# Linear attention and a gated MLP on one core: transposed blocks copied as fp32 words, a second identity, wider engine choices and a new order table

## The chip, the cores and the metric

The kernel runs on one core of a Trainium2 chip. The core has five engines with queues of their own: TensorE (PE in the profile) multiplies, VectorE (DVE), ScalarE (ACT) and GpSimd (POOL) work on tiles, and SyncE (SP) issues nearly all DMAs here. TensorE writes only to PSUM, eight banks of which serve as one ring; DVE and ACT read PSUM, POOL does not. The metric is the device time in microseconds; less is better.

## The reference

Four batches, eight heads, 768 steps, head size 48. First a gated recurrence per head, then a two-layer MLP whose second half is normalised and mixed over the sequence:

```python
for t in range(S):
    state = alpha[:, :, t, :, None] * state + np.einsum('bhd,bhe->bhde', k[:, :, t], v[:, :, t])
    y[:, :, t] = np.einsum('bhd,bhde->bhe', q[:, :, t], state)
# x = y as (4, 768, 384)
h = np.maximum(x @ w_in, 0.0)                      # w_in: 384 x 1024
u, v = (h[..., :512].copy(), h[..., 512:].copy())
v_n = (v - mean(v)) / np.sqrt(var(v) + 1e-06)      # over the last axis
v_s = np.einsum('ts,bsd->btd', w_spatial, v_n) + b_spatial[None, :, None]
out = (u * v_s) @ w_out                            # w_out: 512 x 384
```

## The kernel before, in words

The sequence of a batch is cut into six chunks of 128 steps, 24 chunks in all, numbered i. Within a chunk the recurrence becomes matmuls. The first eight chunks are handled in four pairs (`pair`, numbered j: chunks 2j and 2j+1, interleaved by parity `par`), the other sixteen one by one (`first`). The steps of a pair, by the names that the table of operations gives them:

- `ac`, `kc`, `qc`, `vc`: four loads, 384 KB each for a pair, 192 KB for a single chunk.
- `lnp`: ACT takes the logarithm of alpha (L443). `cump` j par: two matmuls on a triangle matrix sum the logarithms (L452). `einvp` and `eexpp`: ACT takes exp of minus the sum and of the sum (L460, L469).
- `ktp` (k times the first, L474, POOL before) and `qtp` (q times the second, L481, DVE).
- `tr` k/q: four transposes through a PSUM bank against the identity `ident` (L502). `ev` k/q: that bank is copied to SBUF as `kqT` (L198 on ACT, L200 on DVE: both lines belong to the helper `copy`).
- `sc`: score matmuls (L574), `m`: DVE multiplies the scores with a mask (L585), `ya` and `y`: matmuls to the chunk's output (L601, L614).
- `updq`, `z`, `S`, `sb`: the state of 128x192 fp32. TensorE makes the update (L544), DVE adds the old state (`z`, L328 and L330), `S` multiplies with the decay (L335), `sb` copies it to bf16 (POOL).
- `xs`, `xt`, `xe`: the output is copied to SBUF, transposed (L365 for pairs, L389 for single chunks) and copied out of PSUM as `xT`, the MLP's input.

Single chunks have the same steps as `ln`, `cum`, `einv`, `eexp`, `kt`, `qt`, `trk`, `ev`, `sc`, `m`, `y` (L651 to L773). The MLP per batch: `v` (six tiles of three 512-column matmuls, then relu to `v_sb`), `bn` (mean and variance), `rs` (one over the deviation), `vn` (the normalised tile, L916), `u` (eight groups of three matmuls, then relu), `s` (eight groups of six 384-column matmuls on `vn` and the transposed `w_spatial`, then DVE adds the bias, L967), `g` (product with u, L980), `o` (six groups of four matmuls) and `st` (the stores). All big matmul groups are issued at L819. Weights come as fp32 (`raw_w`) and are cast to bf16 by `cast`; `w_spatial` is transposed by `wt` and copied by `we`.

The order of everything is written out by hand: `PLAN` lists one word per operation, with a letter for the engine and the operation's number, and `replay` emits the operations in that order. Each engine runs its own instructions strictly in that order, SP its DMAs too; semaphores make an instruction wait for its inputs and for its PSUM bank. Each operation has a table of engines it may be given to (`ENGINES` and dictionaries beside the calls of `op`). Numbers behind a PE word (`P118:512:512:192`) are filler: that many columns of fp32 matmul on a constant tile `junk`, put into the bank just ahead of the real matmuls (L188).

Before, the first words issue the loads `ac` 0, `ac` 2, `kc` 0, `vc` 0, `qc` 0, `qc` 2, `kc` 2, `w_in` 1, `vc` 2, `ac` 4; a load is numbered by the first chunk of its pair, so that `ac` 2 belongs to pair 1. The first `cump` is that of pair 1. Filler of 512, 512 and 192 columns stands ahead of it, 512, 512, 512 ahead of the first `tr`, 504 ahead of the first `sc` and 512 ahead of the first `ya`.

Of the kernel before, what the change touches and what calls it, by code (L numbers as in the profile page):

```python
# [36 lines left out]
class Slot:  # L37
# [7 lines left out]
    "S": {"POOL": 0.5},  # L45
    "sb": {"POOL": 0.73, "DVE": 0.95},
    "vn": {"DVE": 0.42},
    "xe": {"ACT": 0.4},
# [9 lines left out]
D0 S49 Q50 D7 D13 S109 Q110 G47 Q48 D11 S51 Q52 G9 D3 S55 Q56 D1 G8 D15 D17 G14 D6 D4 D2 D12 G16 S53 Q54 A57 S113 Q114  # L58
G18 A117 P118:512:512:192 S111 Q112 P68 A119 P262 A69 P58 S19 Q20 P264 G71 A59 P128 A120 A60 G61 S115 Q116 A70 D62
A129 D72 A265 D5 S178 Q179 A263 D122 A130 P126:512:512:512 D132 S180 Q181 G131 P76 P74 P64 P66 D75 G63 A65 D77 G73 D67  # L60
D127 G121 P89:504 P134 S182 Q183 D90 P136 P78 A135 D91 A137 P86 S184 Q185 G133 D80 A23 P124 D88 P149 A79 A125 G81 D87
A123 S322 Q323 G22 D83 A186 P92:512 D151 G82 P146 D93 G21 P96 P187 D150 A97 G84 P197 S24 Q25 A188 P94 D148 P138 G85
A95 D147 A189 G190 P98 S326 Q327 P100 A198 D191 A99 G200 A199 D140 P103 S324 Q325 A101 D201 G202 P195 A139 A192 D102
P203 G141 P193 A104 P205 P207 G142 D143 A194 D196 A206 P152 G144 D204 S29 Q30 D105 A330 S382 Q383 G145 P153 P157 P215
A154 D158 G10 P212 A208 A106 D209 P155 P341 D213 A156 G210 P159 P331 D214 A160 P161 A332 D216 G28 P172 A342 D217 G211
A333 A343 D335 G27 P218 A173 D345 G26 A162 P223 P219 D174 P349 A224 P339 S33 Q34 G334 P170 A220 S328 Q329 D350 P225
D163 P221 S384 Q385 P166 G344 A226 A222 P164 D167 A175 P337 P230 D171 A165 A338 D107 P227 D177 A231 D108 S386 Q387
P168 A390 D176 D340 A228 D32 P347 A169 P238 D31 A348 D229 P247 A239 P244 P362 S37 Q38 A245 P236 D248 A246 D249 G35
P240 D364 A237 S424 Q425 P242 A346 D363 G336 A241 P250 G36 D232 P391 A252 P351 A393 A243 D251 S426 Q427 P253 A233 D353
P270 A392 D234 P266 S428 Q429 A352 A255 D235 G354 P274 D254 A395 P275 D356 G355 D396 P271 G394 D276 P267 D272 S388  # L70
# [54 lines left out]
def kernel(  # L125
# [76 lines left out]
    def relu(eng, out, in_):  # L202
        if eng == "ACT":
            nc.scalar.activation(out=out, in_=in_, func=AF.Relu)  # L204
        else:
            ENG[eng].tensor_scalar_max(out=out, in0=in_, scalar1=0.0)
# [953 lines left out]
```

## Time and profile before

| | us |
|---|---|
| median of three runs | 141.43 (141.38 to 141.93) |
| span of the profiled execution | 144.3 |
| TensorE busy in it | 136.8 (95%) |
| VectorE busy | 118.7 (82%) |
| ScalarE busy | 106.8 (74%) |
| GpSimd busy | 86.8 (60%) |

The page gives no other time for the profiled execution than its span, which runs from its first to its last instruction and is 2.9 us above the median of the runs. Busy time of an engine is the union of its instructions' spans; matmuls are pipelined, so that a row of 326 ns for a 384-column matmul says how long one takes from start to end, not how far apart two of them start.

### The profile page before, as it was taken

To read this page: it belongs to the slowest core of one execution; us is meant where nothing else is said; L and a number is where in the kernel's file an instruction comes from. 1 tells how busy PE (TensorE), PEld (TensorE's weight loads), DVE (VectorE), ACT (ScalarE), POOL (GpSimd) and SP (SyncE) were. 2 spreads that over 40 slices of the span, in tenths; PEclk is the share of its full clock that TensorE was granted. 3 is DMA by queue.
4 is the path that set the end of the run, shared out by engine and by line. 5 is a ranking of instruction groups with operands and counts; after the bars stand their busy time and mean duration, and the time that the engine had idled before them with its cause. 6 is when DMAs were issued, how large, how long until landed. Compare 5 with 4: busy or idle time off the path is not lost.

```text
span 144.3 us, 4963 instructions
## 1 busy us (share of the span) xinstructions
PE 136.8 (95%) x1915; PEld 84.2 (58%) x1915; DVE 118.7 (82%) x289; ACT 106.8 (74%) x278; POOL 86.8 (60%) x152
## 2 busy tenths in 40 slices
PE   7799999799799999999999999999999999999990
PEld 3334766656465765676556665665657666555560
DVE  7015798899999969899999999999979897987940
ACT  3473479899895879899997789998797698861031
POOL 6856179892709979981249789511599687002820
PEclk9999999999999999999999999999999999999998
DMA  4999999929899989999899899799999241090055
GB/s 108 321 326 351 282 250 325 344 58 259 181 269 191 300 164 182 205 181 214 169 211 222 175 174 185 152 204 196 212 239 227 66 172 55 0 354 28 5 191 191
DMA packets 89000, 28.64 MB, mean 198 GB/s; under 512 B 83728, under 2 KB 87440, under 8 KB 88976
## 3 DMA queue, kind: packets, MB, share of 16 engines
q1 hardware_dynamic: 88944, 28.32, 79.5%
q8 instruction: 15, 0.25, 0.7%
q14 instruction: 9, 0.07, 0.1%
q0 software_dynamic: 32, 0.00, 0.0%
HBM read 23.60 MB, written 4.72 MB: 196 GB/s over the span
## 4 chain that ended last, share of the span: by engine, by line
PE 78%; DVE 8%; ACT 5%; DMA 3%; issue 3%; SPq 0%; ACTq 0%; DVEq 0%
PE bank L819 47%; PE bank L188 4%; DMA ac<-in_alpha_dram 3%; PE bank L710 3%; PE bank L452 2%; PE bank L502 2%; PE bank L745 2%; PE bank L574 2%; DVE ptm L756 2%; PE bank L773 2%; PE bank L731 2%; PE bank L544 1%; DVE ptm L585 1%; PE bank L657 1%; PE bank L601 1%
## 5 line engine op out<-in xcount | busy, mean ns | idle before, releaser
L819 PE MATMUL bank<-w_spT,vn 128*128 128x384 bf16 x192 | 36.3, 326 | 0.1
L980 POOL TENSOR_TENSOR gT<-vsb,uT 128x384 bf16<-128x384 f32 x28 | 25.7, 927 | 11.7 <-DVE vsb L967 11.2
L335 POOL TENSOR_TENSOR state<-state,bc 128x192 f32<-128x192 f32 x20 | 10.3, 513 | 21.4 <-DVE state L328 6.2
L819 PEld LDWEIGHTS <-vn 128*128 128x128 bf16 x192 | 17.1, 97 | 10.2 <-issue 0.2
L756 DVE TENSOR_TENSOR ptm<-bank,mask 128x512 bf16<-128x512 f32 x32 | 20.8, 682 | 1.0 <-ACT xT L198 1.0
L819 PE MATMUL bank<-xT,w_in 128*128 128x384 bf16 x96 | 19.4, 326 | 0.0
L967 DVE TENSOR_TENSOR vsb<-bank,bsp_bc 128x384 f32<-128x384 f32 x31 | 16.7, 554 | 3.2 <-PE bank L819 2.8
L819 PE MATMUL bank<-w_in,xT 128*128 128x512 bf16 x72 | 18.8, 379 | 0.0
L198 ACT COPY kqT<-bank 128x512 bf16<-128x512 bf16 x24 | 13.6, 590 | 6.9 <-PE bank L502 4.4
L819 PE MATMUL bank<-w_out_sb,gT 128*128 128x384 bf16 (+1 forms) x100 | 18.4, 320 | 0.1
L681 POOL TENSOR_TENSOR kt<-kc,binv 128x384 bf16<-128x384 f32 x13 | 12.0, 927 | 6.6 <-ACT bc L676 2.7
L200 POOL CAST sbd<-state 64x192 bf16<-64x192 f32 x40 | 13.6, 341 | 2.1
L884 DVE BATCH_NORM_STATS2 stats<-v_sb 128x6 f32<-128x512 bf16 x20 | 13.6, 681 | 0.5 <-ACT v_sb L204 0.5
L204 ACT ACTIVATE v_sb<-bank 128x512 bf16<-128x512 f32 x20 | 11.9, 608 | 1.6 <-PE bank L819 1.6
L198 ACT CAST x_sb<-bank 128x384 bf16<-128x384 f32 x21 | 10.2, 493 | 3.5 <-PE bank L773 2.7
L819 PEld LDWEIGHTS <-w_in 128*128 128x128 bf16 x96 | 8.7, 97 | 6.0
L188 PE MATMUL bank<-junk 128*128 128x512 f32 (+2 forms) x16 | 11.1, 838 | 1.1 <-DVE halves_of L264 1.1
L200 DVE COPY kqT<-bank 128x512 bf16<-128x512 bf16 x24 | 9.2, 415 | 3.1 <-PE bank L502 2.3
L819 PEld LDWEIGHTS <-gT 128*128 128x128 bf16 x100 | 8.7, 97 | 5.1 <-POOL gT L980 0.2
L204 ACT ACTIVATE uT<-bank 128x384 bf16<-128x384 f32 x23 | 11.3, 495 | 0.3 <-PE bank L819 0.2
L198 ACT COPY xT<-bank 128x192 bf16<-128x192 bf16 (+1 forms) x27 | 9.1, 378 | 2.4 <-PE bank L365 1.5
L585 DVE TENSOR_TENSOR ptm<-bank,mask 128x512 bf16<-128x512 f32 x16 | 10.2, 682 | 0.7 <-PE bank L574 0.4
(128 smaller groups left out, 285.2 us busy)
## 6 DMA issues: line engine op xcount, KB each, us to landing
ac<-in_alpha_dram SPq DMA_DIRECT2D x16, 192.0 KB, 3.9
kc<-in_k_dram SPq DMA_DIRECT2D x16, 192.0 KB, 4.2
qc<-in_q_dram SPq DMA_DIRECT2D x16, 192.0 KB, 4.0
vc<-in_v_dram SPq DMA_DIRECT2D x16, 192.0 KB, 3.8
raw_w<-in_moe_w_spatial_dram SPq DMA_DIRECT2D x3, 768.0 KB, 4.5
out_dram<-raw_w SPq DMA_DIRECT2D x11, 192.0 KB, 2.0
out_dram<-o_sb SPq DMA_DIRECT2D x9, 192.0 KB, 1.9
ac<-in_alpha_dram SPq DMA_DIRECT2D x4, 384.0 KB, 5.5
```

What stands on the lines that cost most here:

```text
L188: nc.tensor.matmul(out=flat[:, 0:cols].rearrange("p (a b) -> p a b", a=4), lhsT=junk, rhs=junk[:, None, 0:n].to_broadcast([128, 4, n]), st ...
L198: nc.scalar.copy(out=out, in_=in_)
L200: ENG[eng].tensor_copy(out=out, in_=in_)
L204: nc.scalar.activation(out=out, in_=in_, func=AF.Relu)
L335: ENG[eng].tensor_tensor(out=st["state"], in0=st["state"], in1=st["bc"][:, :, None].to_broadcast([128, HP, D]), op=ALU.mult)
L585: nc.vector.tensor_tensor(out=st[f"ptm{par}"][:, s], in0=st[f"pt{s}{par}"], in1=mask2[:, par], op=ALU.mult)
L681: ENG[eng].tensor_mul(out=k_blocks(kt3)[:, :, :, 0:D], in0=quad(st["kc"]), in1=st["binv"])
L756: nc.vector.tensor_tensor(out=st["ptm"][:, s], in0=st[f"pt{s}"], in1=mask4, op=ALU.mult)
L819: return lambda ps: nc.tensor.matmul(out=out(ps), lhsT=lhsT(), rhs=rhs(), start=start, stop=stop)
L884: nc.vector.bn_stats(out=stats, in_=d["v_sb"][:, tt, :])
L967: nc.vector.tensor_tensor(out=hold["vs"], in0=ps[:, 0:TH], in1=bsp_bc[:, th, :], op=ALU.add)
L980: ENG[eng].tensor_tensor(out=bt[b]["gT"][:, dsl, cols], in0=hold["vs"], in1=bt[b]["uT"][:, dsl, cols], op=ALU.mult)
```

## The change

Six things change at once.

1. `copy_pairs`: where a transposed bf16 block leaves PSUM (`ev`, `xe`, `we`) and the engine is ACT, input and output are viewed as fp32, so that a 128x512 block is copied as 128x256 words. On DVE the copy is as before.
2. `ident_q`: a permuted identity, made by one more POOL copy behind `ident`. `xt` of the pairs transposes against it, so that the columns come out in the order in which `xT` keeps them, and `xe` of the pairs copies straight instead of with a stride.
3. `ENGINES`: `S` may also go to DVE, `vn` also to POOL (two POOL instructions, a 128x1 and a 128x512 one), `xe` of pairs and `v` also to DVE.
4. `b_sp_sb` no longer has a tile of its own but lies in `w_spT`.
5. `c_id` issues the extra copy.
6. `PLAN` is another table with the same 1156 words.

By the new table `vn` is 16 times on POOL and 8 times on DVE (24 on DVE before), `S` 12 times on DVE and 8 on POOL (20 on POOL before), `ev` 38 times on ACT and 10 on DVE (24 and 24 before), `v` 5 times on DVE (all 24 on ACT before), `ktp` 3 of 8 times on DVE, `g` 25 times on POOL and 6 on DVE (28 and 3), `vb`/`vbp` 10 times on POOL (14 before), the casts of `w_sp` 4 times on POOL and 2 on ACT (3 POOL, 2 DVE, 1 ACT). The loads come in the order `ac` 2, `ac` 0, `qc` 0, `kc` 0, `qc` 2, `vc` 0, `kc` 2, `ac` 4, `qc` 4, `vc` 2, `w_in` 1, `kc` 4. Filler is 3008 columns in 24 pieces (3768 in 8 before): 1152 columns in six pieces ahead of the first `cump` (pair 1's again), the rest in pieces of 64 to 256 columns, 640 of it in six pieces between that `cump` and the first `tr`. The order of the first DVE steps after the loads is `ktp` 0, four `qtp`, a bias copy, `ktp` 1, then `z`, `S`, `z` and the masks of pair 0; ACT's is the eight exponentials (a bias copy among them), a `vb` cast, and `ev`.

```diff
 ENGINES = {
     "kt": {"POOL": 0.9, "DVE": 0.47},
     "vb": {"POOL": 0.48, "ACT": 0.42, "DVE": 0.27},
-    "S": {"POOL": 0.5},
+    "S": {"POOL": 0.5, "DVE": 0.35},
     "sb": {"POOL": 0.73, "DVE": 0.95},
-    "vn": {"DVE": 0.42},
-    "xe": {"ACT": 0.4},
+    "vn": {"DVE": 0.42, "POOL": 0.75},
+    "xe": {"ACT": 0.4, "DVE": 0.3},
...
 PLAN = """
-D0 S49 Q50 D7 D13 S109 Q110 G47 Q48 D11 S51 Q52 G9 D3 S55 Q56 D1 G8 D15 D17 G14 D6 D4 D2 D12 G16 S53 Q54 A57 S113 Q114
-G18 A117 P118:512:512:192 S111 Q112 P68 A119 P262 A69 P58 S19 Q20 P264 G71 A59 P128 A120 A60 G61 S115 Q116 A70 D62
+S109 Q110 D0 D2 G47 Q48 D13 D15 G14 S49 Q50 D17 D3 D6 D12 D5 G18 S53 Q54 D4 D1 D11 A117 S51 Q52 G9 G16
+P118:384:320:64:128:128:128 A57 S113 Q114 A119 A120 S55 Q56 P58:64:128 A59 P128:128 P68 A60 S111 Q112 D61 P262 A69 A70
...
+    def copy_pairs(eng, out, in_):
+
+        copy(eng, *((out.bitcast(FP32), in_.bitcast(FP32)) if eng == "ACT" else (out, in_)))
+
...
+    ident_q = consts.tile([128, 128], BF16, name="ident_q")
...
-    b_sp_sb = consts.tile([1, S], BF16, name="b_sp_sb")
     wsp_nat = [None] * NT
     w_spT = consts.tile([128, NT, NT, 128], BF16, name="w_spT")
+    b_sp_sb = w_spT[0:1, 0].rearrange("p n t -> p (n t)")
...
-                    nc.tensor.transpose(xv[:, ks, :], st["x_sb"][:, ks, :], ident)
+                    nc.tensor.transpose(xv[:, ks, :], st["x_sb"][:, ks, :], ident_q)
...
-                copy(eng, bt[b]["xT"][:, c].rearrange("p k (t two) -> p k t two", two=2),
-                     st["xv"].rearrange("p k (two t) -> p k t two", two=2))
+                copy_pairs(eng, bt[b]["xT"][:, c], st["xv"])
...
-                        copy(eng, st["kT"][:, par], hold["t"])
+                        copy_pairs(eng, st["kT"][:, par], hold["t"])
...
-                copy(eng, st["kqT"][:, :, 64 * r:64 * r + 64], hold[r])
+                copy_pairs(eng, st["kqT"][:, :, 64 * r:64 * r + 64], hold[r])
...
-                    copy(eng, w_spT[:, tt, :, 64 * r:64 * r + 64], hold[r])
+                    copy_pairs(eng, w_spT[:, tt, :, 64 * r:64 * r + 64], hold[r])
...
-              {"ACT": 0.61 if on_act else 0.48}, None, [made.get(("vn", b - 2, tt))], parts=1)
+              {"ACT": 0.61} if on_act else {"ACT": 0.48, "DVE": 0.6}, None, [made.get(("vn", b - 2, tt))], parts=1)
...
+    def c_id(_):
+        make_identity(nc, ident)
+        nc.gpsimd.tensor_copy(
+            out=ident_q.rearrange("p (t a) -> p a t", a=2), in_=ident.rearrange("p (a t) -> p a t", a=2))
+
+    op(("c_id",), "POOL", 0.5, c_id, prio=-19.0)
```

More of the change, by code (lines that the diff above doesn't have):

```diff
@@ L396, in xe @@
                     tiles(b)
[L397 removed]
+                copy_pairs(eng, bt[b]["xT"][:, c, :, 64 * r:64 * r + 64], to[r])
             made[("xe", i)].append(op(
@@ L517, in ev @@
                                 "p a h c -> p (a h c)").rearrange("p (h c a t) -> p h c a t", a=2, c=2, h=HP)
-                        copy(eng, st["qT"][:, :, :, par, :], hold["t"].rearrange("p h (c t) -> p h c t", c=2))
+                        copy_pairs(eng, st["qT"][:, :, :, par, :], hold["t"].rearrange("p h (c t) -> p h c t", c=2))
                 op(("ev", nm, j, par), EV, None, ev,
```

100 lines of the change are left out of this document (49 added, 51 removed).

## The prediction

> **What bounds the kernel now.** I read the page first (busy shares and the chain that ended last), then stretches of time, then the chain itself, and last the timeline and the groups of instructions.
>
> ```profile
> span 144.3 us, 4963 instructions
> PE 136.8 (95%) x1915; PEld 84.2 (58%) x1915; DVE 118.7 (82%) x289; ACT 106.8 (74%) x278; POOL 86.8 (60%) x152
> ...
> PE 78%; DVE 8%; ACT 5%; DMA 3%; issue 3%; SPq 0%; ACTq 0%; DVEq 0%
> ```
>
> ```profile
> 0.00:23.30 23.30, 21.06 (x248) 11.06 (x249) 12.99 (x41) 13.05 (x26) 14.43 (x34) 1.00 0.97 275
> 23.30:40.00 16.70, 14.99 (x264) 9.84 (x263) 15.37 (x36) 14.82 (x38) 12.16 (x22) 1.00 0.79 224
> 40.00:123.50 83.50, 83.24 (x1300) 52.79 (x1299) 77.08 (x184) 71.64 (x195) 55.30 (x92) 1.00 0.87 188
> 123.50:141.10 17.60, 17.54 (x113) 10.46 (x109) 13.30 (x31) 6.94 (x21) 4.90 (x5) 1.00 0.34 124
> ```
>
> The columns of a stretch are its length, busy PE, PEld, DVE, ACT and POOL, the granted clock, the DMA share and GB/s. From 40 us on PE idles 0.3 us in 101: this part is bound by the matmuls, which the change leaves as they are. What can move lies ahead of 40 us. There the chain (start, length, what) shows filler, waits for the first loads, and then DVE:
>
> ```profile
> 1.23 4.23 DMA ac<-in_alpha_dram
> ...
> 6.38 1.44 PE bank L452 x4
> 7.82 0.43 PE bank L848
> ...
> 10.17 4.25 PE bank L188 x6
> 14.43 1.12 PE bank L502 x20
> 15.55 0.90 PE bank L188 x2
> 16.45 0.35 PE bank L574 x16
> ...
> 19.06 1.05 PE bank L188 x2
> 20.11 0.51 PE bank L601 x32
> ...
> 21.25 0.65 PE bank L452 x4
> ...
> 23.48 1.39 PE bank L819 x6
> ...
> 29.46 1.89 DVE ptm L585 x3
> ...
> 35.37 1.84 DVE vn L916 x4
> ...
> 37.54 1.25 DVE w_row L200 x2
> ```
>
> L188 is the filler: 6.2 us on the chain between 10 and 20 us. `ya` of the first pair (L601) starts at 20.11, the first big group (`v`, L819) at 23.48. In 23.3 to 40 us DVE is busy 15.37 of 16.70, and PE loses 1.7 us.
>
> **The change, part by part.** *The start.* The two alpha loads change places:
>
> ```profile
> 1.06 4.42 PE L188 MATMUL bank<-junk 128*128 128x512 f32 x6 [1.06 <-DVE halves_of L264]
> ...
> 4.24 0.84 ACT L443 ACTIVATE la<-ac 128x768 bf16<-128x768 f32 x1 [2.21 <-DMA ac<-in_alpha_dram]
> ...
> 5.48 0.84 ACT L443 ACTIVATE la<-ac 128x768 bf16<-128x768 f32 x1 [0.40 <-DMA ac<-in_alpha_dram]
> ...
> 6.63 1.15 SPq L432 DMA_DIRECT2D kc<-in_k_dram  x1
> ...
> 7.83 1.15 SPq L1084 DMA_DIRECT2D raw_w<-in_moe_w_in_dram  x1
> ```
>
> The first `cump` is pair 1's. Before, pair 1's alpha comes second and `cump` waits to 6.38; after, it comes first, its logarithm ends at 5.08. Six instructions took 4.42 us for 1216 columns, 3.6 ns a column; 1152 columns are 4.2 us, to 5.25. So `cump` starts there, 1.1 us earlier. The steps that follow cost by these groups (busy, mean ns | idle):
>
> ```profile
> L198 ACT COPY kqT<-bank 128x512 bf16<-128x512 bf16 x24 | 13.6, 590 | 6.9 <-PE bank L502 4.4 <-PE bank L710 2.1 <-DVE w_row L200 0.4
> L335 POOL TENSOR_TENSOR state<-state,bc 128x192 f32<-128x192 f32 x20 | 10.3, 513 | 21.4 <-DVE state L328 6.2 <-ACT v_sb L870 4.6 <-DVE vn L916 3.7
> L585 DVE TENSOR_TENSOR ptm<-bank,mask 128x512 bf16<-128x512 f32 x16 | 10.2, 682 | 0.7 <-PE bank L574 0.4 <-issue 0.3
> L200 DVE COPY kqT<-bank 128x512 bf16<-128x512 bf16 x24 | 9.2, 415 | 3.1 <-PE bank L502 2.3 <-ACT o_sb L198 0.5
> L330 DVE TENSOR_TENSOR state<-bank,state 128x192 f32<-128x192 f32 x16 | 5.6, 352 | 0.3
> L198 ACT COPY xT<-bank 128x192 bf16<-128x192 bf16 x19 | 5.3, 335 | 0.9 <-PE bank L389 0.9
> L481 DVE TENSOR_TENSOR qt<-qc,bank 128x384 bf16<-128x384 f32 x8 | 4.2, 545 | 7.1 <-ACT bank L469 7.1
> L460 ACT ACTIVATE binvp<-bank 128x384 bf16<-128x384 f32 x8 | 3.8, 494 | 1.7 <-PE bank L452 1.6
> L198 ACT COPY xT<-bank 128x384 bf16<-128x384 bf16 x8 | 3.7, 480 | 1.5 <-PE bank L365 1.5
> ```
>
> PE: four `cump` at 0.72 (half of 1.44), two bias matmuls at 0.43, 640 columns of filler at 3.6 ns: 6.1 us, so the first transposes stand at 11.35 instead of 14.43. ACT: nine instructions at 0.49 from 6.32, with some 0.7 lost waiting for the fourth `cump`: the last exponential ends at 11.4, the last `qtp` at about 12.0. The first scores need three transposed banks and three ACT copies. A word copy costs what 256 columns cost: between 335 (192) and 480 (384), 0.38 us; the bounds are 0.335 and the 0.590 of today. Banks from about 12.0, copies to 13.1, scores of par 0 to 13.5, of par 1 to 14.0. DVE meanwhile does `z`, `S`, `z` at 0.35 from 13.1, then four masks at 0.68: 14.2 + 2.7 = 16.9. `ya` at 17.0 instead of 20.11: **3.1 us** earlier. `v` stands 3.4 us behind `ya` (23.48 - 20.11) and would come at 20.4, if `w_in` is there:
>
> ```profile
> raw_w<-in_moe_w_in_dram SPq DMA_DIRECT2D x2, 768.0 KB, 6.5
> ```
>
> (KB each, median us from issue to landing.) It is now behind ten loads instead of seven. Issues follow each other every 1.2 us (6.63 to 7.83), so it is issued at 7.83 + 3.6 = 11.4, lands at 17.9, and with its three casts side by side on DVE, ACT and POOL (0.61 to 0.63 each) `v` can start at 18.6: 1.8 us of cover. If the queue makes it 3 us later than that, 1.2 of the 3.1 are lost. I keep 3.1, as the path through `ya` is the later one, with 1.9 as the low end. 1216 columns of filler stand behind the first transpose's place. They cost nothing as long as they lie in waits: between 11.35 and 17.0 the walk gives TensorE some 3.5 us of work (eight banks 1.8, four scores 1.4, the update), so 2 us of waits are there. At the later rate of 0.90 us for 504 columns they are 2.2 us, which would be lost if nothing waited; the old filler of this stretch (6.2 us on the chain) is gone from the walk in exchange.
>
> *23 to 40 us.* Five of the first batch's six `vn` leave DVE for POOL and both `w_row` casts leave it: the chain's 1.84 and 1.25 us. PE's loss there is 1.7 in all; I take **1.0**, between 0 (the masks, 1.89, stay, and `S` is added) and 1.7.
>
> *Whole budgets.* DVE: 16 `vn` less at 0.43 (-6.9), 14 `ev` less (-5.8), 12 `S` more at 0.35 (+4.2), 5 relus of `v` more at 0.68 as for a mask (+3.4), the rest +2.0: about -3 us. ACT: 14 `ev` more at 0.38 (+5.3), 24 shorter by 0.21 (-5.0), 27 `xT` copies shorter by 0.07 to 0.15 (-2.5), five relus less (-3.0), the rest +2: about -3. POOL carries what DVE gave:
>
> ```profile
> L200 POOL CAST w_in<-raw_w 128x512 bf16<-128x512 f32 x5 | 3.0, 610 | 0.1
> L200 POOL CAST w_row<-raw_w 128x768 bf16<-128x768 f32 x3 | 2.5, 826 | 3.2 <-DMA raw_w<-in_moe_w_spatial_dram 2.8 <-DVE w_row L200 0.5
> L980 POOL TENSOR_TENSOR gT<-vsb,uT 128x384 bf16<-128x384 f32 x28 | 25.7, 927 | 11.7 <-DVE vsb L967 11.2
> L916 DVE TENSOR_SCALAR vn<-v_sb,mvs,rstd 128x512 bf16<-128x512 bf16 x24 | 9.2, 430 | 0.9 <-ACT rstd L909 0.6
> ```
>
> No row has this on POOL. One tensor input like the cast: 0.61; the narrow instruction ahead of it as the cast's part that does not grow with columns (0.84 ns a column between 512 and 768), 0.18: 0.79, against 0.43 on DVE. At the two-input rate of L980 (2.41 ns a column) it would be 1.24 + 0.18 = 1.42. I take 0.79, as it reads one tensor. 16 of them are +12.6; 12 `S` less -6.2, `g`, `vb` and `k` products -5.8: POOL stays near 60%. Ahead of the `s` that needs it stand 0.6 us of matmuls (batch 0) to 1.6 (batch 3) behind the last of a row of POOL `vn`; that is the cover. From 40 us on I count nothing gained: PE idles 0.3 us there.
>
> The Trainium skill (GPSIMD Engine Reference, Engine selection) puts elementwise work on VectorE and calls GpSimd about twice as slow with two tensor inputs and near line rate with one. By the one-input half of that rule the 0.79 and the sum stand; if the two per-partition scalars made it an instruction of two inputs, the sum would be that of the slower rival below. No run here shows which.
>
> The extra `ident_q` copy (POOL, 0.3 at most by the cast rows) lies before 7 us, ahead of transposes at 11: free. The bias row in `w_spT` is read before the first `we`: free.
>
> Sum: 3.1 + 1.0 = 4.1. The profiled execution (144.3, 2.9 above the median) becomes 140.2; the median **137.3**.
>
> **Rivals.** *Loads set the pace: smaller gain.* For: the DMA share is 0.97 up to 23.3 us. Against: 1.8 us of cover. With `w_in` 3 us late the start gives 1.9, the sum 2.9: 138.5; without the gain of the second part 139.5.
>
> *The clock stays low: smaller gain.* The same four matmuls (L452) took 1.44 us at 6.38 and 0.65 at 21.25, though the clock column says 1.00 for both; the filler likewise: 4.25 us for six instructions at 10.17, 0.90 for two at 15.55. So TensorE runs at about half speed until between 10 and 15.5 us. In the walk above, transposes (0.22 a bank by 1.12 us for five), scores (0.35 a par) and the update before 17 us are priced fast. If they are slow, three banks and two scores on the path cost 1.4 more, and later filler twice what it should: 1.4 to 2.4 lost, 138.7 to 139.7. The Trainium skill (TensorE: Matmul & The Clock Gate, Part 1) has the array at half rate until a window of some 3.4 us has been busy, and half rate again after an idle one; by that rule filler in small pieces between waits may fail to fill a window, and the time would be the 138.7 to 139.7. The rows agree that it is slow early and fast after 4 us of unbroken filler.
>
> *POOL decides: slower.* In batches 0, 2 and 3 four or five `vn` stand in a row on POOL ahead of `s`. Each 0.1 us above 0.79 delays the last of a row by 0.4. The 4.1 us are gone at 4.1 / (3 x 4) = 0.34 above, at 1.13 us each; at 1.42 it is 3 x 4 x 0.63 = 7.6 lost, 144.9. For: L980's rate; against: the cast's, and a cover of 0.6 to 1.6 us.
>
> *Larger gain.* If all 6.2 us of filler on the chain, the 1.1 of the first load and the 1.7 of the second part went, it were 9.0: 132.4. Half way from the forecast is 134.9.
>
> **How the numbers follow.** Forecast (136.0 to 138.5) 0.45; smaller gain by the loads 0.10, by the clock 0.10 (both to 140.7); larger 0.15; no change 0.05; slower 0.15. Half a per cent is about what a measurement tells from no change. Faster 0.80, same 0.05, slower 0.15. The range 134.6 to 141.6 reaches past the half-way point of the larger gain (0.05 beyond) and leaves out most of the slower case (0.13).
>
> **What would show it.** First L452 at 5.3, first L601 at 17, first L819 by 20.5; ACT `kqT` rows of 256 columns at 0.38; POOL `vn` at 0.6 and a narrow row at 0.2; in 23 to 40 us `vn` and `w_row` off the chain. Wrong, if the chain shows POOL `vn` ahead of L819, or DMA `raw_w` ahead of the first L819.

## The result and the profile after

The changed kernel takes 144.89 us, the median of four executions (144.82 to 145.09), against 141.38 to 141.93 in three of the four executions of before beside it: a ratio of 1.025, with a 95% interval of 1.023 to 1.026. It is slower by 3.4 us, where I forecast 4.1 faster. One plain fact is needed for what follows: executions of the kernel before lie between 141.3 and 145.5 us, and the ratios compare those near the lowest, while the profile on which I built the prediction was of a long one.

From the page of the changed kernel, the busy times and the chain's shares:

```profile
span 143.0 us, 5050 instructions
...
PE 134.6 (94%) x1947; PEld 86.9 (61%) x1947; DVE 118.6 (83%) x280; ACT 102.4 (72%) x291; POOL 93.6 (65%) x165
...
PE 52%; DVE 15%; DMA 10%; POOL 8%; SPq 7%; issue 5%; ACT 0%; POOLq 0%; DVEq 0%
```

The time of this execution, 144.82, is its span and 1.8 us. TensorE's share of the chain fell from 78 to 52%; loads, VectorE and POOL took its place. The first three of the same four stretches as before (length, busy PE, PEld, DVE, ACT, POOL, granted clock, DMA share, GB/s):

```profile
0.00:23.30 23.30, 21.33 (x368) 16.55 (x368) 17.06 (x51) 17.19 (x41) 13.56 (x32) 1.00 1.00 285
23.30:40.00 16.70, 16.26 (x272) 10.52 (x261) 15.00 (x36) 14.88 (x43) 14.64 (x28) 1.00 1.02 296
40.00:123.50 83.50, 80.99 (x1222) 50.43 (x1219) 74.98 (x171) 64.65 (x198) 57.97 (x97) 1.00 0.80 169
```

Before, TensorE was busy 83.24 of the 83.50 us from 40 us on, and I counted nothing there. Now it is idle 2.5 us in that stretch. The chain (start, length, what) shows by whom:

```profile
11.46 6.85 DMA raw_w<-in_moe_w_in_dram
...
20.44 7.87 DMA kc<-in_k_dram
...
30.74 1.55 POOL w_row L200 x2
...
32.64 0.77 POOL vn L929
33.40 0.45 POOL vbp L200
34.19 0.77 POOL vn L929
35.30 0.77 POOL vn L929
36.07 0.78 POOL w_row L200
...
97.59 1.26 POOL vn L929
```

POOL is on it from 30.7 to 36.9 us with 0.1 us between, and again at 97.6. The groups that answer my prices (busy, mean ns | idle before):

```profile
L198 ACT COPY kqT<-bank 128x256 f32<-128x256 f32 x38 | 13.6, 385 | 2.2 <-PE bank L714 1.7 <-DVE vsb L971 0.2 <-DVE qt L485 0.2
L929 POOL TENSOR_SCALAR vn<-v_sb,rstd,nb 128x512 bf16<-128x512 bf16 x16 | 13.1, 818 | 1.6
...
L340 DVE TENSOR_TENSOR state<-state,bc 128x192 f32<-128x192 f32 x12 | 5.5, 461 | 1.1 <-ACT bc L554 0.7
...
L926 POOL TENSOR_SCALAR nb<-mvs,rstd 128x1 f32<-128x1 f32 x16 | 4.2, 265 | 7.0 <-ACT rstd L913 4.4 <-ACT rstd L912 2.6
```

The word copy costs 0.385, as said (0.38). A `vn` on POOL costs 0.82 and 0.27 instead of 0.61 and 0.18. On POOL's timeline of the changed kernel (start, length) the next one begins 1.10 us behind the one before, not 0.79:

```profile
96.11 0.26 POOL L926 TENSOR_SCALAR nb<-mvs,rstd 128x1 f32<-128x1 f32 x1
96.47 0.77 POOL L929 TENSOR_SCALAR vn<-v_sb,rstd,nb 128x512 bf16<-128x512 bf16 x1
97.21 0.26 POOL L926 TENSOR_SCALAR nb<-mvs,rstd 128x1 f32<-128x1 f32 x1
97.57 1.27 POOL L929 TENSOR_SCALAR vn<-v_sb,rstd,nb 128x512 bf16<-128x512 bf16 x1
```

The last of these is the fourth of batch 2's five. It takes 1.27 us while VectorE, on its own timeline, makes a `vn` and a `kt`:

```profile
97.50 0.40 DVE L920 TENSOR_SCALAR vn<-v_sb,mvs,rstd 128x512 bf16<-128x512 bf16 x1
97.81 0.55 DVE L685 TENSOR_TENSOR kt<-kc,binv 128x384 bf16<-128x384 f32 x1
```

On TensorE's timeline of the changed kernel, the first `cump`, the first `ya`, the first `v`, and the wait for that fourth `vn` (in brackets the idle time and its releaser):

```profile
5.04 0.32 PE L456 MATMUL bank<-la,le_pair 128*128 128x384 bf16 x1
...
15.74 0.79 PE L605 MATMUL bank<-vbp,ptm 64*128 64x48 bf16 x32
...
19.75 1.46 PE L823 MATMUL bank<-w_in,xT 128*128 128x512 bf16 x6
...
98.90 0.66 PE L823 MATMUL bank<-w_spT,vn 128*128 128x384 bf16 x3 [1.88 <-POOL vn L929]
```

### The profile page after: what moved, and what is told of

Read it like the earlier page. It is cut to its first block, busy times and chain, and to the rows that moved or that the text cites. A ratio compares the mean times of both kernels' runs of the same rounds, so it can differ in the third digit from the quotient of the medians.

```text
span 143.0 us, 5050 instructions
## 1 busy us (share of the span) xinstructions
PE 134.6 (94%) x1947; PEld 86.9 (61%) x1947; DVE 118.6 (83%) x280; ACT 102.4 (72%) x291; POOL 93.6 (65%) x165
## 4 chain that ended last, share of the span: by engine, by line
PE 52%; DVE 15%; DMA 10%; POOL 8%; SPq 7%; issue 5%; ACT 0%; POOLq 0%; DVEq 0%
PE bank L823 39%; SPq L436 7%; DMA kc<-in_k_dram 6%; DMA raw_w<-in_moe_w_in_dram 5%; POOL vn L929 4%; DVE ptm L760 4%; PE bank L714 2%; DVE stats L888 2%; PE bank L749 2%; PE bank L735 2%; POOL w_row L200 2%; PE bank L661 2%; DVE o_sb L200 1%; PE bank L777 1%; DVE vsb L971 1%
## 5 line engine op out<-in xcount | busy, mean ns | idle before, releaser
L984 POOL TENSOR_TENSOR gT<-vsb,uT 128x384 bf16<-128x384 f32 x25 | 23.2, 945 | 6.8 <-DVE vsb L971 6.2
L760 DVE TENSOR_TENSOR ptm<-bank,mask 128x512 bf16<-128x512 f32 x32 | 20.7, 682 | 0.9 <-PE bank L749 0.7
L685 POOL TENSOR_TENSOR kt<-kc,binv 128x384 bf16<-128x384 f32 x15 | 13.6, 916 | 9.7 <-ACT binv L673 5.4
L200 POOL CAST sbd<-state 64x192 bf16<-64x192 f32 x40 | 13.7, 344 | 7.2 <-DVE state L340 5.3
L198 ACT COPY kqT<-bank 128x256 f32<-128x256 f32 x38 | 13.6, 385 | 2.2 <-PE bank L714 1.7
L929 POOL TENSOR_SCALAR vn<-v_sb,rstd,nb 128x512 bf16<-128x512 bf16 x16 | 13.1, 818 | 1.6
L888 DVE BATCH_NORM_STATS2 stats<-v_sb 128x6 f32<-128x512 bf16 x20 | 13.7, 683 | 0.2
L188 PE MATMUL bank<-junk 128*128 128x128 f32 (+4 forms) x48 | 10.8, 349 | 1.1 <-DVE junk L1054 1.1
L673 ACT ACTIVATE binv<-bank 128x384 bf16<-128x384 f32 x16 | 7.9, 493 | 5.3 <-PE bank L664 2.4
L198 ACT COPY raw_w<-bank 128x384 f32<-128x384 f32 x9 | 4.3, 485 | 9.8 <-PE bank L823 9.8
L208 ACT ACTIVATE v_sb<-bank 128x512 bf16<-128x512 f32 x15 | 9.0, 599 | 2.1 <-PE bank L823 2.1
L695 DVE TENSOR_TENSOR qt<-qc,bank 128x384 bf16<-128x384 f32 x16 | 8.5, 549 | 2.3 <-ACT bank L690 2.0
```

The costliest lines, as they stand in the source:

```text
L188: nc.tensor.matmul(out=flat[:, 0:cols].rearrange("p (a b) -> p a b", a=4), lhsT=junk, rhs=junk[:, None, 0:n].to_broadcast([128, 4, n]), st ...
L198: nc.scalar.copy(out=out, in_=in_)
L200: ENG[eng].tensor_copy(out=out, in_=in_)
L685: ENG[eng].tensor_mul(out=k_blocks(kt3)[:, :, :, 0:D], in0=quad(st["kc"]), in1=st["binv"])
L760: nc.vector.tensor_tensor(out=st["ptm"][:, s], in0=st[f"pt{s}"], in1=mask4, op=ALU.mult)
L888: nc.vector.bn_stats(out=stats, in_=d["v_sb"][:, tt, :])
```

## The experiments

Times are the median with the lowest and highest; ratios are to the kernel before in the same session.

**What the profile of before was of.** First the kernel before once more, unchanged.

> The kernel before, profiled once more. The changed kernel has the shorter span (143.0 against 144.3) and the longer time (144.89 against 141.4). Theory A: the profile of before caught an execution in which TensorE ran at half speed until 13.4 us; usual executions are fast from about 5 us on. Then this profile has a span of about 139.6 (141.4 less the 1.8 us by which the changed kernel's time stands above its span), the first four L452 take about 0.7 us instead of 1.44, and ya (first L601) starts near 17, not at 20.1. Rival B: the profile was usual, and the changed kernel carries 3 to 4 us outside its span (before the first or after the last instruction). Then the span is 144 again and the first L601 at 20.

Measured: 142.73 (141.32 to 145.32, ten executions). The profiled execution was again a long one, 145.32 with a span of 143.5. Span and time differ by 1.8 us in it as in all others, so rival B falls, though a long span and a late `ya` were its signs: nothing is hidden outside the span. By the same 1.8 us I estimate the execution that I had used, with its span of 144.3, at 146.1 us, 4.7 above the median. The timeline of TensorE in the new profile:

```profile
6.37 0.48 PE L452 MATMUL bank<-la,le_pair 128*128 128x384 bf16 x1 [0.89 <-ACT la L443]
...
9.96 4.52 PE L188 MATMUL bank<-junk 128*128 128x512 f32 x6
```

Six filler instructions take 4.52 us: half speed up to 13.5 us, and `ya` at 20.10. Then the same kernel with the filler ahead of the first `cump` made longer, which shortens TensorE's pause there from 0.9 to 0.5 us:

```diff
-P118:512:512:192
+P118:512:512:512
```

> The kernel before with 512:512:512 instead of 512:512:192 columns of filler ahead of the first cump, so that TensorE has no gap between 5.5 and 6.4 us. Both profiles of before show it at half speed until 13.4 us, and its unprofiled times spread from 141.3 to 145.4. Theory A: the spread is the moment at which TensorE comes up to speed, which needs some 3.4 us without a gap; the bridge makes that moment come before 8 us: times bunch at 141.0 to 141.8 and a profile at 143 or less with ya before 18.5. Rival: the spread has another cause (loads, another user of the memory): times spread as before, 141.3 to 145, and the added filler costs up to 0.5.

Measured: 141.51 (141.32 to 143.18, ten of eleven up to 141.92), where the kernel before beside it spread from 141.27 to 145.45; ratio 0.999 (0.996 to 1.003). The best level is the same, and the executions of 144 and 145 us are gone: in this kernel most of the spread goes with TensorE's rate at the start. It is not all of it: the eleventh, the profiled one, took 143.18 with TensorE fast from 6.4 us, and waited 0.87 us for `qt` at 12.1 instead.

A profile of before with TensorE fast from 6.5 us on came from a run on the loads, in which two thirds of the bytes of `w_in` are left out and the casts read the block that is there:

```diff
-            nc.sync.dma_start(out=hold["w"], in_=src)
+            if key[0] == "w_in":
+                nc.sync.dma_start(out=hold["w"][:, 0:1], in_=src[:, 0:1])
+            else:
+                nc.sync.dma_start(out=hold["w"], in_=src)
...
-                copy(eng, wsp_nat[tt] if to is None else to[:, j, :], hold["w"][:, j, :])
+                copy(eng, wsp_nat[tt] if to is None else to[:, j, :], hold["w"][:, 0 if key[0] == "w_in" else j, :])
```

> The kernel before with the same third of w_in (the product with w_in is another one). In its profile loads land 1 to 5 us ahead of their use. Theory L: not paced by loads, so within 0.5 us of 141.4 in its fast runs. Rival: the old table is paced by them as well, and gains as much as the new one: 139 or less.

Measured: 141.58 (141.33 to 146.20), ratio 0.997 (0.992 to 1.003): fewer bytes give nothing. Its profiled execution took 141.56 with a span of 139.8. TensorE's timeline:

```profile
6.46 0.32 PE L452 MATMUL bank<-la,le_pair 128*128 128x384 bf16 x1 [1.39 <-ACT la L443]
...
8.50 2.74 PE L188 MATMUL bank<-junk 128*128 128x512 f32 x6
...
17.04 0.57 PE L601 MATMUL bank<-vbp,ptm 64*128 64x48 bf16 x32
...
20.05 1.56 PE L819 MATMUL bank<-w_in,xT 128*128 128x512 bf16 x5
```

The same six filler instructions take 2.74 us, `ya` starts at 17.04 and `v` at 20.05. In the profile that I used they stood at 20.05 and 23.32 in this view (20.11 and 23.48 in its chain). Of the 3.1 us that I forecast as the gain of the start, 3.0 are what a half-speed start costs the old kernel at `ya`; executions without it never had them to lose.

From here on this is the profile to compare with, called undisturbed. Its smaller loads do not matter for that: the profile with the longer filler, whose loads are whole, has the same matmuls 1.5 to 1.6 us later all the way from 18 to 110 us. I give every matmul the step of its shape in steady state (0.162 us for 384 columns, 0.2155 for 512 and so on, filler nothing; 116.75 us in all), and read when a given amount of this work had begun. The two tables order the matmuls differently, so the steps taken for the small ones matter: others move a single difference by up to 0.5. The last two columns have the same order and can be compared without this doubt.

| work done, us | before, undisturbed | changed | difference | changed, batch 2's `vn` on DVE |
|---|---|---|---|---|
| 8 | 19.93 | 18.89 | -1.04 | 18.93 |
| 20 | 33.62 | 32.84 | -0.78 | 32.88 |
| 36 | 50.68 | 50.66 | -0.02 | 50.60 |
| 64 | 81.03 | 80.81 | -0.22 | 80.75 |
| 68 | 85.25 | 86.09 | +0.84 | 86.04 |
| 76 | 94.02 | 94.89 | +0.87 | 94.83 |
| 80 | 98.14 | 100.86 | +2.72 | 98.96 |
| 116 | 135.66 | 138.90 | +3.24 | 137.38 |

By this table the changed kernel does start 1.0 us ahead. It loses that lead by 50 us, then 1.06 us between 81 and 86, 1.85 at 97 and 0.5 behind 100. The last column is of an experiment below.

**Loads.** The `w_in` load is on the chain of the changed kernel. In one run it is issued as the eighth load instead of the eleventh; in another it has a third of its bytes:

```diff
-S178 Q179 ... S182 Q183 ... S19 Q20
+S19 Q20 S178 Q179 ... S182 Q183
```

> The changed kernel with the load of w_in issued eighth, as before, instead of eleventh; nothing else moves. Theory L: the first 20 us are paced by the loads and w_in is the one waited for (the chain goes through it, landing at 18.3): its cast comes 3 us earlier and v with it; the three loads behind it come 2.4 us later and push back pair 2. 143.5 to 144.5. Rival P: the loss lies behind 30 us, on POOL: 144.7 to 145.

> The changed kernel with a third of the bytes of both w_in loads (one of three blocks is loaded and cast three times; the product with w_in is therefore another one). Theory L: the loads pace the first 30 us of the new table (nearly every load is used within 0.15 us of its landing): 1 MB less is some 3 us less of loading, 2 to 3 us of it seen: 142 to 143. Rival P: what is lost lies behind 30 us: 144.4 to 145.

Measured: the earlier load makes it slower, 147.91 (145.85 to 150.96), ratio 1.031 (1.022 to 1.041), which neither theory had; in the profiled execution TensorE falls back to half speed twice, from 16.0 to 19.4 and from 29.6 to 33.0 us. With a third of the bytes (the edit shown for the old kernel): 145.14 (144.12 to 146.46), ratio 1.020 (1.004 to 1.037); the two better executions gain 0.7 on the changed kernel. In the profiled one TensorE is 0.4 us ahead of the changed kernel from 37 to 99 us, and then loses 1.7 to one stretch of 3.4 us at half speed. So loads take 0.4 to 0.7 us, and most of the 3.4 went elsewhere.

**The order table and the words.** First the changed kernel's code with the whole `PLAN` of before:

> The changed kernel's code (word copies, second identity) with the old order table, so old engines and old filler. Theory: word copies alone help a little: 27 xT copies and 24 kqT copies on ACT shorter by 0.07 to 0.2 us, ACT is rarely on the path: 140.5 to 141.5. Rival: the extra POOL copy at the start or the second identity costs: 141.5 to 142.

Then the changed kernel with ScalarE's copies made as bf16 again:

```diff
-        copy(eng, *((out.bitcast(FP32), in_.bitcast(FP32)) if eng == "ACT" else (out, in_)))
+        copy(eng, out, in_)
```

> The changed kernel with ScalarE's copies of transposed blocks made as bf16 elements again; everything else of the change stays. ScalarE gets 38 x 0.2 us for kqT and some 2.5 us for the others, 10 us in all, from 102 to 112 busy. If the word copies do their work off the path (theory H): 144.6 to 145.2, no change. If the new order needs them (theory W), a third or more of the 10 us shows: 147 to 151, with ScalarE's copies kqT and xT among what the matmuls wait for.

Measured: with the old table 141.56 (140.81 to 144.43), ratio 0.997 (0.992 to 1.001); the lowest is 0.5 below the lowest of before beside it. So the words, the second identity and the bias row cost nothing that shows, and the loss is the new table's. Without the words the new table needs 149.6 (149.46 to 149.94), ratio 1.055 (1.049 to 1.060): 4.7 of the 10 us that ScalarE gets show. The waits of TensorE in that run (us in total, times, longest):

```profile
PE bank L823 <- POOL vn L929: 1.7, 2, 1.2
...
PE bank L823 <- DVE state L335: 0.8, 3, 0.4
PE bank L749 <- ACT kqT L198: 0.7, 2, 0.5
PE bank L823 <- ACT xT L198: 0.6, 2, 0.4
```

ScalarE's copies `kqT` and `xT` are on the list, as theory W wanted. The new order leans on the words; with the old one they show by 0.5 us at most.

**`vn` on POOL.** A word of the table is an engine's letter and a step's number (G is POOL, D VectorE, A ScalarE). All `vn` put back on VectorE, then POOL's two instructions made one, then batch 2's five alone put back, then batch 0's five as well:

```diff
-G107 G177 G108 G176 G235 G381 G460 G662 G742 G741 G661 G808 G943 G942 G1022 G1021
+D107 D177 D108 D176 D235 D381 D460 D662 D742 D741 D661 D808 D943 D942 D1022 D1021
```

> The changed kernel with all 24 vn on DVE, as before; the places in the table stay, 16 letters change. Theory P: POOL's vn (0.82 + 0.27 us measured, a wait of 2.0 us on the chain at 97 us, and the chain through POOL at 32 to 37 and 124 to 127 us) are most of the loss: 142 or less. Rival D: DVE is as full as POOL is late, and moving them back only moves the wait: within 0.5 us of 144.9, or above it.

Measured: 144.92 (144.35 to 146.87), ratio 1.018 (1.013 to 1.022): at most 0.5 of it comes back, as rival D said. In the profiled execution (146.87) TensorE ran at half speed for one window right after a thin stretch; by stretches of time (columns as above):

```profile
36.00:40.20 4.20, 2.70 (x74) 1.80 (x73) 4.20 (x10) 2.89 (x10) 1.74 (x2) 0.98 0.88 209
40.20:43.60 3.40, 3.40 (x12) 1.58 (x11) 1.70 (x6) 0.56 (x2) 0.00 (x0) 0.52 1.05 257
```

VectorE is busy all 4.20 us of the first, TensorE 2.70 of it. VectorE has no room there.

```diff
-                nb = small.tile([128, 1], FP32, name="nb")
-                nc.gpsimd.tensor_scalar(
-                    out=nb, in0=d["mvs"][:, t, 0:1], scalar1=d["rstd"][:, t:t + 1], scalar2=-1.0,
-                    op0=ALU.mult, op1=ALU.mult)
                 nc.gpsimd.tensor_scalar(
-                    out=d["vn"][:, t, :], in0=d["v_sb"][:, t, :], scalar1=d["rstd"][:, t:t + 1], scalar2=nb,
-                    op0=ALU.mult, op1=ALU.add)
+                    out=d["vn"][:, t, :], in0=d["v_sb"][:, t, :],
+                    scalar1=d["mvs"][:, t, 0:1], scalar2=d["rstd"][:, t:t + 1],
+                    op0=ALU.subtract, op1=ALU.mult)
```

> The changed kernel, with POOL's vn made by one instruction (subtract the mean, times rstd, as on DVE) instead of a narrow one and a wide one. Table and engines stay. Measured, a POOL vn takes 1.10 us from start to start (0.27 + 0.77 and a gap). Theory P: the narrow one and its gap are what the table has no room for; 0.33 us less for each, five in a row at 94 to 99 us: the wait of 1.9 us ahead of L823 there shrinks by 1.3 to 1.6, and 143.0 to 143.8. Rival D: DVE or the loads hold the same stages: 144.5 or more.

Measured: 162.18 (161.67 to 163.21), ratio 1.145 (1.130 to 1.159). The one instruction is dearer by far than the two, as the group shows:

```profile
L925 POOL TENSOR_SCALAR vn<-v_sb,mvs,rstd 128x512 bf16<-128x512 bf16 x16 | 33.5, 2097 | 6.1 <-ACT rstd L913 3.5 <-ACT rstd L912 2.6
```

and TensorE's first wait (us in total, times, longest):

```profile
PE bank L823 <- POOL vn L925: 10.0, 4, 5.4
```

Against the 1.10 us of the pair that is 1.0 more for each, 16 us for sixteen, and 17.3 us of time. I had not expected the price of this form, and which part of it is dear, the subtraction or the other scalars, is not shown. Theory P is not tested by it, but the run shows that a longer `vn` on POOL makes TensorE wait. Not all of the 17.3 us is waiting: TensorE also ran at half speed for 13.7 us in all, in three stretches of the profiled execution.

```diff
-G662 G742 G741 G661 G808
+D662 D742 D741 D661 D808
```

> The changed kernel with the five vn of batch 2 that it has on POOL put on VectorE; the other eleven stay on POOL. Theory T (the loss is made of single waits in the new order): the 1.88 us that the matmuls wait at 97 us for the fifth POOL vn of this batch goes, VectorE takes 5 x 0.43 = 2.1 us more near there and gives 0 to 0.5 of it back: 142.9 to 143.4, and no wait of over 0.5 us on a vn in 90 to 100. Rival M (the order is paced by all engines together, and a wait that is taken away comes back elsewhere, as with all 24 on VectorE): 144.3 or more, with a new wait of 1 us or more on a VectorE step between 90 and 110.

Measured: 143.56 (143.27 to 144.51), ratio 1.013 (1.006 to 1.020). The wait (for the fourth `vn` of the row, not the fifth) of 1.88 us at 97 us is gone (the last column of the table: the 1.85 lost there become 0.01), and 1.5 of it stay to the end (1.3 by the medians). This wait alone is some 1.5 of the 3.4 us; theory T holds for it.

```diff
-G107 G177 G108 G176 G235
+D107 D177 D108 D176 D235
```

> The kernel with batch 2's vn on VectorE, and the five vn of batch 0 there too; six of 24 stay on POOL. Theory T (the lead of the start is lost between 24 and 45 us to the row of POOL vn, which the chain shows from 32 to 36): 142.3 to 143.0. Rival V (VectorE is as full there, 11.3 of 13 us between 32 and 45, and has no room for five more at 0.43): 143.3 to 145.5, with waits on a VectorE step between 30 and 45 us; the loss of the kernel with all vn on VectorE then comes from this batch.

Measured: 146.65 (144.51 to 147.28), ratio 1.029 (1.016 to 1.042), with a mean clock of 0.988 in three of four executions (in the profiled one, half speed for 3.4 us from 40 us on). The fourth, 144.51 at 0.998, is still 1.0 above the run without this edit, and in the profiled one 1.4 us are lost before the clock falls. So theory T falls for batch 0, and V holds. The profiled execution with all `vn` on VectorE loses its time in the same place and gains 2.0 at batch 2.

**The state scalings on VectorE.** All twelve back on POOL, then one of them narrowed to one column, then the two that collide back on POOL, and two `xT` copies moved from VectorE to ScalarE:

```diff
-D81 D141 D210 D354 D357 D482 D613 D726 D894 D928 D965 D1044
+G81 G141 G210 G354 G357 G482 G613 G726 G894 G928 G965 G1044
```

> The changed kernel with the twelve state scalings that moved to VectorE back on POOL. Theory S (these twelve, at 0.46 us each beside POOL work instead of the 0.35 that I took, make the loss of 0.9 us between 80 and 86): 143.9 to 144.2. Rival P (POOL is the scarce engine of the new order; 12 x 0.51 = 6.2 us more on it delay its vn further): 145.5 to 148, with POOL vn and POOL state in the list of what TensorE waits for.

Measured: 147.99 (145.94 to 148.53), ratio 1.044 (1.036 to 1.051). The wait list:

```profile
PE bank L823 <- POOL vn L929: 2.2, 2, 2.0
...
PE bank L823 <- DVE state L335: 1.0, 2, 0.8
```

The time is in rival P's range and POOL's `vn` leads the list, though POOL's `state` is not on it. Four of the five executions have a mean clock of 0.986 to 0.988; the profiled one, at 0.997, took 145.94, 1.0 more than the changed kernel. POOL has no room for them. Yet the work from 64 to 68 took 4.79 us instead of 5.28, so theory S was right about that stretch, 0.5 us of it. In the changed kernel VectorE's scaling there and the `kt` on POOL's timeline are these:

```profile
82.56 0.92 DVE L340 TENSOR_TENSOR state<-state,bc 128x192 f32<-128x192 f32 x1
```

```profile
81.49 1.78 POOL L685 TENSOR_TENSOR kt<-kc,binv 128x384 bf16<-128x384 f32 x2
```

The next run, on top of batch 2's `vn` on VectorE, asked why:

```diff
+            w = 1 if i == 15 else D
+            h = 1 if i == 15 else HP
             ENG[eng].tensor_tensor(
-                out=st["state"], in0=st["state"], in1=st["bc"][:, :, None].to_broadcast([128, HP, D]),
-                op=ALU.mult)
+                out=st["state"][:, 0:h, 0:w], in0=st["state"][:, 0:h, 0:w],
+                in1=st["bc"][:, 0:h, None].to_broadcast([128, h, w]), op=ALU.mult)
```

> The kernel with batch 2's vn on VectorE, in which the one scaling of the state of chunk 15 (the state row of 0.92 us at 82.56 in the changed kernel) is cut to one column of 192, so that this decay is left out for the rest. Theory D (between 79 and 86 us VectorE and POOL both have no gap, and this stretch loses 0.8 to 1.0 us because VectorE got more there): at least half of the 0.92 comes back, 142.4 to 142.8, and the matmuls' steps from 81 to 86 shorten by as much. Rival Q (the stretch is set by POOL's kt and gT, or by the order itself): 143.2 to 143.4, as without the cut.

Measured: 143.11 (142.91 to 143.60), ratio 1.012 (1.009 to 1.016), 0.4 below the run without the narrowing. Theory D wanted at least 0.46 of time, which leaves it undecided by the time; the matmuls from 84 to 86 us come 0.5 earlier, as it wanted, and 0.3 of that is left at the end. VectorE's and POOL's timelines tell more:

```profile
82.61 0.73 DVE L342 TENSOR_TENSOR state<-state,bc 128x1 f32<-128x1 f32 x1
83.27 0.55 DVE L986 TENSOR_TENSOR gT<-vsb,uT 128x384 bf16<-128x384 f32 x1
```

```profile
81.55 1.78 POOL L687 TENSOR_TENSOR kt<-kc,binv 128x384 bf16<-128x384 f32 x2
83.27 0.90 POOL L200 CAST vb<-vc 128x384 bf16<-128x384 f32 x1
```

One column takes 0.73 us and ends as POOL's pair of `kt` ends, at 83.33; then POOL's cast (0.63 in the changed kernel) takes 0.90 beside VectorE's `gT`. By these lengths each waits for the other.

```diff
-D613 D726
+G613 G726
```

> The kernel with batch 2's vn on VectorE, and two state scalings (chunks 12 and 15, VectorE rows of 0.77 and 0.92 us at 72.45 and 82.56) put back on POOL. In the run with the narrow scaling, one column still took 0.73 us and ended as POOL's two kt ended: it stood waiting, not working. Theory C (VectorE's scaling cannot run beside POOL's kt, so it holds up all of VectorE behind it): VectorE gets 0.77 + 0.92 us back, POOL takes 2 x 0.51; the matmuls' stretch from 81 to 86 us shortens by 0.5 to 0.9, and the time is 142.4 to 142.8. Rival Q (POOL sets that stretch): 143.2 to 144.0, longer than without the edit.

Measured: 143.48 (143.06 to 144.19) (no ratio; the kernel before stood at 141.67 to 145.54 beside it). The work from 64 to 68 took 4.79 us, 0.5 less, as theory C wanted, but the time did not follow: in the profiled execution 0.6 us were lost earlier, at a wait of 1.0 us for POOL's `w_row`, and 0.3 of the 0.5 went again at once, to a wait for POOL's `gT` on TensorE's timeline:

```profile
86.74 0.82 PE L823 MATMUL bank<-w_out_sb,gT 128*128 128x384 bf16 x4 [0.26 <-POOL gT L984]
```

So rival Q, that POOL sets the stretch, holds as well. And the next VectorE instruction with two inputs in SBUF took over the wait, on VectorE's timeline:

```profile
82.58 0.35 DVE L335 TENSOR_TENSOR state<-bank,state 128x192 f32<-128x192 f32 x1
82.85 1.27 DVE L984 TENSOR_TENSOR gT<-vsb,uT 128x384 bf16<-128x384 f32 x1
```

The first of these two reads a bank and SBUF and keeps its 0.35 in the middle of POOL's `kt` (81.92 to 83.71 there); the second reads SBUF twice and takes 1.27 instead of the 0.55 of the run with the narrow scaling (0.85 in the changed kernel).

```diff
-D655 D656
+A655 A656
```

> The kernel with batch 2's vn on VectorE, and the two copies of chunk 13's transposed x (VectorE at 80.16 and 81.53, 0.25 each) made by ScalarE, which stands idle for 1.17 us before 80.41. Theory D (VectorE sets the stretch from 79 to 86): 0.3 to 0.5 less, 142.8 to 143.0. Rival Q: 143.2 to 143.5, no change, or a later ScalarE step on the path.

Measured: 143.75 (142.86 to 144.06), ratio 1.015 (1.010 to 1.020); the stretch did not shorten (5.30 us). Rival Q holds here: VectorE's 0.5 us of copies do not set the stretch.

**The lead lost between 20 and 50 us.** POOL's four `w_row` casts given to ScalarE, and then both edits together:

```diff
-G32 G31 G35 G40
+A32 A31 A35 A40
```

> The kernel with batch 2's vn on VectorE, and the four casts of w_spatial rows that POOL makes between 30.7 and 40.0 us (0.8 each) made by ScalarE, which has 4.8 us free between 32 and 45. Theory P (POOL's row of casts and vn, on the chain from 30.7 to 36.9, takes the lead of the start): the POOL vn of batch 0 end 1.6 to 3 us earlier and 0.5 to 0.9 us of the time comes back, 142.4 to 142.8. Rival V (VectorE or ScalarE set that stretch too): 143.2 or more, with waits on a ScalarE or VectorE step between 28 and 42 us.

> Both edits of the two runs before. If both theories hold and their places are apart (72 to 86 us and 30 to 40 us), the gains add: 141.6 to 142.2, which with the 1.5 of batch 2's vn leaves some 0.3 to 0.9 of the 3.4 us without a place. If either is refuted, the time is that of the other alone.

Measured: 144.57 (144.52 to 144.97) and 144.49 (144.40 to 145.14), 1 us worse than without the casts' move. From the chain of the first of them:

```profile
31.39 0.72 ACT w_row L198
32.11 0.39 ACT uT L208
32.92 0.72 ACT w_row L198
33.64 0.50 ACT v_sb L208
34.16 0.71 DVE stats L888
```

ScalarE takes POOL's place on the chain, and loses more. Theory P falls as a remedy: the free time that I counted for ScalarE lay behind 36 us, not where the casts stand.

**A version that beats both?** The best that came out is the new code with the old table and the longer filler:

```diff
-P118:512:512:192
+P118:512:512:512
```

> The changed kernel's code with the order table of before, and in that table the first filler's last piece of 192 columns made 512. The longer filler alone brought the times of before together at 141.3 to 141.9; the word copies with the old table had 140.81 as their fastest. Both together, if they add (theory B): 140.6 to 141.2 in nearly every execution, a ratio of 0.990 to 0.996. If the word copies are hidden altogether (rival): 141.3 to 141.9 as with the filler alone, a ratio of 0.997 to 1.001.

Measured: 142.04 (140.97 to 145.15, twelve executions), ratio 0.998 (0.994 to 1.002). Three of twelve (140.97 to 141.17) are 0.2 to 0.4 below the best of before beside it (141.36), but times up to 145.15 are back, which the longer filler alone had removed. Theory B wanted nearly every execution at 140.6 to 141.2, so it does not hold. The two longest have a mean clock of 0.988, as executions with one later stretch at half speed have; why such stretches come back is open.

## Why the prediction was wrong

**The step that failed first is the sum's base.** I wrote "the profiled execution (144.3, 2.9 above the median) becomes 140.2; the median 137.3", and so took the 2.9 us as a constant between profile and runs. They were the profiled execution's own loss, 4.7 us by the estimate above: 3.0 by `ya` and 3.3 by `v` from TensorE's half-speed start, and 1.3 more from waits between 27 and 39 us. My walk of the start priced filler at 3.6 ns a column up to 11.35 us, and then full-rate matmuls behind it, and set the result against a `ya` that half-rate matmuls had delayed; 3.0 of the 4.1 us are that comparison (`ya` at 20.05 in that execution, 17.04 in the undisturbed one, 15.74 after the change). I had the rows in hand: the rival on the clock quoted 1.44 and 0.65 us for the same four matmuls. I asked what a low clock would do to the changed kernel, not whether the median executions of before had it at all.

*The start.* The first `cump` came at 5.04 (5.3 forecast), `ya` at 15.74 (17.0), `v` at 19.75 (20.4): the kernel came 0.3 to 1.3 us ahead of the walk, and the rival on the clock did not come, as that first `cump` at 0.32 us a matmul shows. Against an undisturbed start the gain is 1.3 us at `ya` and 0.3 at `v`. `w_in` landed at 18.31 (17.9). It stands on the chain ahead of the first `v`, one of the two signs that the prediction named for being wrong, though the chain goes from it through VectorE to the issue of a `kc` load and not to `v`. As a cause it is small, 0.4 to 0.7.

*23 to 40 us.* I forecast 1.0 gained by `vn` and `w_row` off VectorE, out of 1.7 that TensorE loses there. More than half of that loss was the long execution's own: over the same matmuls of the undisturbed profile (20.02 to 35.38 us) TensorE is idle 0.75. `vn` and `w_row` are off VectorE, but POOL stands on the chain in their place from 30.7 to 36.9, and of the lead of 0.78 us at 20 us of work nothing is left at 36. Moving batch 0's `vn` back, or the casts to ScalarE, made it worse; all three engines are busy 14.6 to 15.0 of 16.7 us there. What would have kept the lead stays open, but for the 0.4 us that smaller loads gave.

*POOL `vn`.* Mis-sized: 0.79 forecast, 1.10 from start to start measured. The wide part is 0.82 instead of 0.61, the narrow one 0.27 instead of 0.18. The Trainium skill (GPSIMD Engine Reference, Engine selection) has one-input work on GpSimd near line rate; the trace has 0.82 against VectorE's 0.43, so here it was about half. My rival "POOL decides" had its break-even at 1.13 and gave 144.9 at 1.42. That this equals the result is chance: it counted three batches, four `vn` each at 0.63, against a gain that was not there, while the runs show the wait in one batch, 1.5 us of time, where a `vn` took 1.27 beside VectorE's `vn` and `kt`. The wait there is the prediction's other sign of being wrong, a POOL `vn` ahead of a big group. Why the rows of batches 0 and 3 cost no such wait is not shown.

*From 40 us on I counted nothing.* The old table's rows say that TensorE is hardly ever idle there (0.3 us); they say nothing of the new table, in which TensorE loses 1.06 us at 81 to 86 and 1.85 at 97. This was the second failed step, and it made the kernel slower, where the first only took the gain away: a stretch without idle time in the profile of before has no gain to give, but it can lose.

*`S` on VectorE at 0.35* was priced by a row that reads a PSUM bank and SBUF. The moved one reads SBUF twice. Most of the twelve cost what I said, the median is 0.36; but three, all beside POOL's `kt`, take 0.54, 0.77 and 0.92, and the average is 0.46. What this costs is shown for the stretch of 81 to 86 us: 0.5 of its 1.06. The Trainium skill (SBUF — State Buffer, SBUF: two separate sides) says that a VectorE instruction with two SBUF inputs and a GpSimd instruction that reads SBUF take one pair of ports by turns, each held for a whole instruction. The traces agree: one column 0.73 us beside `kt`, `gT` 1.27 instead of 0.55, and 0.35 unchanged for the instruction that reads a bank. This rule spoke against the change, and I did not weigh it: three of its moves (`S`, `g` and `ktp` to VectorE) set more work of two SBUF inputs beside a busier POOL.

*Words and budgets.* 0.385 against 0.38; ScalarE 4.4 us less (3 forecast), VectorE 0.1 less (3 forecast; the dearer `S` is 1.3 of the difference, the rest is not traced), POOL at 65% (60).

So of the 3.2 us by which the changed profile ends later in the table, 1.85 arise at 97 us, 1.06 at 81 to 86 and 0.5 behind 100, less 0.2 of lead still left at 81; the lead of 1.0 was spent before and only cancelled the gain. The wait at 97 us is shown to be batch 2's `vn` on POOL, and 1.5 of it count at the end. At 81 to 86 us 0.5 is shown to be VectorE waiting for POOL, but only the run with the narrow scaling keeps part of it, 0.3 in the profile and 0.4 by the medians; with the scalings on POOL a wait for POOL's `gT` takes most of it back. The rest, and the lost lead, are placed by the table but not explained by a run.

## What to carry to other kernels

Before a duration is taken from a profile, see whether that execution is like the ones whose median is forecast: the same instructions at two lengths (1.44 and 0.65 us for four matmuls) are the sign, and a difference of 2.9 us between profile and median is a cause to be found, not a constant. Where one engine is the bound with hardly a gap, a new order can gain next to nothing there and can lose, so ask of each moved step what its new engine's neighbours do at that moment. And price a step for VectorE or POOL by a row with the same sources: two inputs in SBUF are another thing than a bank and SBUF.

## What the runs showed of the hardware

- TensorE started at half speed in some executions of before and not in others (the same six filler instructions took 4.52 and 2.74 us). The granted clock's column reads 1.00 through it: the trace's first record of that clock stands at 13.4 and 13.5 us in the two profiles with a half-speed start and at 4.5 in the undisturbed one, and the column shows nothing of the time ahead of it. A later fall shows: stretches of 3.4 us at half speed (one of 6.8) in five experiments. The Trainium skill (TensorE: Matmul & The Clock Gate, Part 1) gives windows of 3413 ns that run freely; the stretches here agree in length.
- On POOL, a 128x512 bf16 instruction with two scalars per partition took 0.77 us (0.82 on average) as multiply by `rstd` and add `nb`, and 2.10 on average as subtract the mean and multiply by `rstd`.
- A VectorE instruction of one column took 0.73 us when POOL's two `kt` were running, and a POOL instruction of 0.77 took 1.27 beside VectorE's `vn` and `kt`.
